# One Strassen block of each row block loaded into w_mod's slots instead of the stage tiles, and some pieces of vector work placed at other chunks

## The chip, the cores and the metric

The kernel runs on one core of one Trainium2 chip. The metric is the device time of one execution in microseconds; the time before is the median of three runs. A profile of one more execution shows where that time goes. Times inside it are counted from the start of its span.

## What is computed

Two residual blocks work on x, a 2048 x 512 array (S x D). The rows `sa, ca, ga, sb, cb, gb` come from `silu(c) @ w_mod`, six slices of 512 columns.

```python
h = layernorm(x) * (1 + ca) + sa
x = x + ga * (Cr @ (h @ Hr.T) - Ci @ (h @ Hi.T))      # DFT over the hidden dim, then over the sequence
h = layernorm(x) * (1 + cb) + sb
z = gelu(h @ w_in)                                    # 1792 columns: z1 | z2, 896 each
g = w_sp @ layernorm(z2) + b_sp[:, None]              # w_sp is 2048 x 2048
x = x + gb * ((z1 * g) @ w_out)
```

`Cr`, `Ci` (2048 x 2048) are the sequence DFT matrices, `Hr`, `Hi` (512 x 512) the hidden ones. All arrays are float32, and the result has to be accurate as float32.

## The kernel before

**Products.** Each float32 operand is split into a rounded high part and the remainder, its low part. `matmul3` (lines 97 to 99) adds three products for every pair: high by high, high by low and low by high. The high part is made by ScalarE (`prep_hi` L266, `hi_unit` L603), the low part by VectorE (`prep_lo` L273, `lo_unit` L607), two steps ahead of the matmuls that use it. The DFT matrices and w_sp must also be turned; VectorE does that from a loaded block with a stream transposition (L538 for the DFT, L231 for w_sp).

**The order of the work is written out by hand.** The kernel is one long list of steps, and every engine executes its own instructions in the order in which they are written. In the DFT a step is called a chunk: 12 matmuls of 128 x 512. `at(n, f, ...)` and `atd(n, f, ...)` hang a piece of work at step n; `run(n)` writes it out right after the matmuls of that step, in the order of registration, and n + 0.5 after the low part of that step. A call hung at a step is therefore not a time: it is a place in the queue of VectorE, ScalarE, SyncE (SP, which issues nearly all loads) and GpSimd (POOL, which issues the stores). A load that waits for its buffer holds every later load on SP.

**The stages.**

| stage | steps | what runs |
|---|---|---|
| a | chunks 0 to 31 | first 512 rows of Cr, Ci by h, plainly |
| t = 1, 2, 3 | 30 chunks each, from 32, 62 and 92 | the other row blocks: 16 chunks of plain products ("k") and 14 of a Strassen-like scheme of seven products ("s") |
| y | 32 chunks from Y0 = 122 | hidden DFT, residual, second layernorm |
| z1, z2 | steps N2 = YE to N2 + 27, then 16 steps to N4 | the two halves of w_in; YE = 154 in chunks |
| w | steps N4 to N4 + 111 | w_sp by z2, seven products in the order 1, 6, 7, 4, 5, 3, 2 |
| o | 16 steps | w_out and the final residual |

Within t the order is: for t = 1 four units of "k" (chunks 32 to 39), 14 chunks "s" (40 to 53), four units "k" (54 to 61); for t = 2 "s" at 62 to 75 and "k" at 76 to 91; for t = 3 "s" at 92 to 105 and "k" at 106 to 121.

**Stage tiles.** A block of 512 x 512 of the DFT matrices is 1 MB, four DMAs by `load_block` (L165). Blocks come through a stream: `src` is the list of all of them, `blocks` holds two buffers with the tag "stage", and `block_done(b)` (called after the second half of block b is turned) loads block b + 2. `CHUNKS` gives the order for t = 1, 2, 3: ("k", t, i) are the four blocks of the plain product, ("s", t, role) the four blocks of the scheme, with roles 11, 12, 21 and 22. `turn_unit(u + 3)` turns a "k" block three units ahead of its use; `turn_s` turns the "s" blocks of t + 1 while t is running, at chunks given in a table. For t = 1 alone the "s" blocks are loaded into another pool, by `load_first`.

**Slots of w_mod.** The pool `raws` has two buffers of 1 MB (`raw(...)`). They hold slices of w_mod (`load_mod`, L310, and `load_columns`), their split copies, the hidden DFT matrices, and pieces of w_sp. A buffer is given to a new tile when, in the written order, its former tile has no reader left; SP then waits until that last reader is done.

**Pieces of w_sp.** The scheme for w_sp needs sums of its quarters. `load_s` (L1055, L1057) loads a piece of 128 rows from three quarters (768 KB in the view of DMAs: one issue of 256 KB and one of 512 KB), `sum_s` computes two sums (L1062, L1063) and then a third (L1066) and stores them (L1069). There are 16 pieces, at the chunks listed in `early`. A fourth sum, for product 3, is made by `load_s4` (L1078) and `sum_s4` (L1082) in eight parts. In the y stage `gate_ht` (L817) multiplies the rows of the hidden DFT matrices by `ga`, and `make_ht` (L827) rounds them.

Of the kernel before, what the change touches and what calls it, by code (L numbers as in the profile page):

```python
# [13 lines left out]
P = 128  # L14
# [5 lines left out]
def fnet_gmlp_kernel(  # L20
# [104 lines left out]
    def at(n, f, *a):  # L125
        fill.setdefault(n, []).append((f, a))
# [6 lines left out]
    def quad(a, r, k):  # L133
        return a[r * Q:(r + 1) * Q, k * Q:(k + 1) * Q]

    TS = (NQ - 1, *range(NQ - 1))
    src = [quad((cr, ci)[j], 0, g) for g in range(NQ) for j in range(2)]
    CHUNKS = {1: (("k", 1, 0), ("k", 1, 1), ("s", 2, 21), ("s", 2, 11), ("s", 2, 12), ("k", 1, 2), ("k", 1, 3), ("s", 2, 22)),
              2: (("s", 3, 21), ("s", 3, 11), ("s", 3, 12), ("k", 2, 0), ("k", 2, 1), ("k", 2, 2), ("s", 3, 22), ("k", 2, 3)),
              3: (("k", 3, 0), ("k", 3, 1), ("k", 3, 2), ("k", 3, 3))}  # L140
    order_b = {}
    for t in range(1, NQ):
        for kind, t_, i in CHUNKS[t]:
            order_b[kind, t_, i] = len(src)
            src.append(quad((cr, ci)[i // 2], t_, i % 2) if kind == "k" else
                       quad((cr, ci)[i % 10 - 1], t_, 1 + i // 10))
    first_s = [quad(cr, 1, 3), quad(cr, 1, 2), quad(ci, 1, 2), quad(ci, 1, 3)]
    NC = len(src)
    src += [None] * (8 * NQ - NC)
    N2 = 4 * len(src)  # L150
    src += [h2_d[t] for t in TS] + h2_d
    FORMS = (1, 2, 6, 7, 4, 5, 3)
# [3 lines left out]
    N4 = N3 + 4 * NQ  # L156
# [5 lines left out]
    def load_block(tile_, a, s0=0, s1=P, engs=(nc.sync,)):  # L162
        v = a.rearrange("(b j) (a s) -> a j b s", j=32, a=4)
        for q in range(4):
            engs[q % len(engs)].dma_start(tile_[32 * q:32 * q + 32, :, s0:s1], v[q][:, :, s0:s1])  # L165
# [134 lines left out]
    def raw(shape, name):  # L300
        return raws.tile(shape, F32, tag="raw", bufs=2, name=name)
# [217 lines left out]
    D1 = 8 * NQ  # L519
    DT = 30  # L520
    Y0 = D1 + 3 * DT
    YE = Y0 + 8 * NQ
# [6 lines left out]
    PH, PL, TP, FT = {}, {}, {}, {}  # L529
# [7 lines left out]
    def turn_pair(dst, st, m):  # L537
        nc.vector.transpose(dst.rearrange("p k (b i) -> p k b i", i=32),  # L538
                            st[:, :, 64 * m:64 * m + 64].rearrange("p b (k i) -> p k b i", k=2))
# [6 lines left out]
    SB = {}  # L546

    def turn_s(t, role, m):

        if m == 0:  # L550
            new_f(t, role)
        if t == 1:
            turn_pair(FT[t, role][:, m], SB[role], m)
        else:
            b = order_b["s", t, role]
            turn_pair(FT[t, role][:, m], stage[b], m)
            if m:
                block_done(b)

    def load_first(role):  # L560
        SB[role] = raw([P, 16, P], f"sb{role}")
        load_block(SB[role], first_s[(21, 11, 12, 22).index(role)])

    def sum_f(t, p, m):

# [479 lines left out]
    def load_s(r, g, b):  # L1045

        if spre:
            t = spre[-1].tile([P, 3, Q], F32, tag="sj", bufs=2, name=f"sj{r}{g}{b}")
        elif n_now[0] not in (85, 86):
            t = raw([P, 3, Q], f"sj{r}{g}{b}")  # L1050
        else:
            t = blocks.tile([P, 3, Q], F32, tag="stage", bufs=2, name=f"sj{r}{g}{b}")
        SJ[r, g, b] = t
        o = r * Q + b * P
        nc.sync.dma_start(t[:, 0], w_sp[o:o + P, g * Q:(g + 1) * Q])  # L1055
        v = w_sp.rearrange("r (j c) -> r j c", j=2)[S // 2 + o:S // 2 + o + P]
        nc.sync.dma_start(t[:, 1:], v[:, :, g * Q:(g + 1) * Q])  # L1057
# [240 lines left out]
    n_now = [0]  # L1298

    def atd(n, f, *a):  # L1300

        at(("d", n) if n < YE else N2 + int(n - YE), f, *a)
# [16 lines left out]
    for s, n in ((8, 10), (9, 10)):  # L1319
        m = n + (s == 9)  # L1320
# [13 lines left out]
        fpool.append(tf.enter_context(pool("fpool", "right")))  # L1334

    for role, l, n, m in ((21, 12, 16, 18), (11, 14, 20, 22), (12, 23, 28.5, 30), (22, 30.5, 35, 36)):
        atd(l, load_first, role)
        atd(n, turn_s, 1, role, 0)
        atd(m, turn_s, 1, role, 1)
    for n, *todo in ((23, (change_f,), (sum_v, 5)), (24, (hi_v, 5)), (25, (lo_v, 5), (sum_v, 7), (sum_v, 6)),  # L1340
# [6 lines left out]
    for t in range(1, NQ):  # L1347
        o = D1 + DT * (t - 1)
        d = 8 if t == 1 else 0
        for m in range(2):  # L1350
            atd(o + d + 0.5 + m, sum_f, t, 6, m)
            atd(o + d + 6 + m, sum_f, t, 3, m)
        for j in range(2):
            atd(o + ((22, 29) if t == 1 else (21, 29))[j], *((out_last, j) if t == NQ - 1 else (out_k, t, j)))
        if t < NQ - 1:
            for role, n, m in (((21, 13, 14), (11, 15.5, 16.5), (12, 17.5, 18.5), (22, 24, 25)) if t == 1 else
                               ((21, 3, 5), (11, 7.5, 8.5), (12, 9.5, 10.5), (22, 21, 23))):
                atd(o + n, turn_s, t + 1, role, 0)
                atd(o + m, turn_s, t + 1, role, 1)
            for p, n, m in (((5, 26, 26.5), (7, 27, 28)) if t == 1 else ((5, 24, 26), (7, 27, 28))):  # L1360
                atd(o + n, sum_f, t + 1, p, 0)
                atd(o + m, sum_f, t + 1, p, 1)
# [7 lines left out]

    atd(33, row_c)
    atd(38, silu_c)
    for j, l, n in ((1, 66, 73), (0, 67, 77)):
        atd(l, load_columns, j)
        for k in range(4):
            atd(n + k, weigh_column, j, k)
            atd(n + k + 1, sum_column, j, k)
    atd(82, scale_columns)
    for j, l, ns, m, k, plus_one in ((2, 37, (40, 41, 42), 44, 6, False), (4, 46, (56, 57, 58), 60, 3, True),
                                     (3, 58.5, (63, 64, 65), 66, 7, False), (5, 78, (82, 83, 85), 87, 0, False)):  # L1380
        atd(l, load_mod, j)
        atd(ns[0], sum_mod, j, [0, 1])
        atd(ns[1], sum_mod, j, [2, 3])
        atd(ns[2], split_mod, j)
        atd(m, spread_mod, j, k, plus_one)
    early = ((43.5, 53), (85.5, 89), (86.5, 91), (109, 113), (117, 120))
    early += tuple((YE + c, YE + c + 4) for c in (14, 17, 20, 23, 27, 29, 31, 33, 35, 37, 38))
    for (n, m), u in zip(early, [(r, g, b) for g in range(2) for b in range(4) for r in range(2)]):
        atd(n, load_s, *u)
        atd(m, sum_s, *u, True)  # L1390
        atd(m + 1, sum_s, *u, False)
    atd(93, load, order_b["k", 3, 0])
    atd(96.5, load, order_b["k", 3, 1])
    hrs = ctx.enter_context(ExitStack())
    o = D1 + 2 * DT
# [9 lines left out]
    for n, *todo in ((-6, (load_ht, 0)), (-3, (turn_ht, 0, 0)), (-2, (turn_ht, 0, 1)), (-1, (turn_ht, 0, 2)), (0, (turn_ht, 0, 3)), (8, (scale_w0, 0)),  # L1405
                     (9, (load_ht, 1), (weigh_ht, 0, 0), (weigh_ht, 0, 1)), (10, (weigh_ht, 0, 2), (weigh_ht, 0, 3), (load_w0, 0)),
                     (12, (fold_ht, 0, 0), (fold_ht, 0, 1)), (13, (fold_ht, 0, 2), (fold_ht, 0, 3)),
                     (14, (open_hr,), (split_acc, 0), (turn_ht, 1, 0), (scale_w0, 1), (read_row, 2, hrp)),
                     (15, (change_y,), (turn_ht, 1, 1), (turn_ht, 1, 2), (read_row, 4, yp), (read_row, 3, yp)),
                     (16, (turn_ht, 1, 3), (weigh_ht, 1, 0), (load_w0, 1)),  # L1410
                     (17, (weigh_ht, 1, 1), (weigh_ht, 1, 2), (load_xr, YORD[0])),
                     (18, (weigh_ht, 1, 3), (load_xr, YORD[1])),
                     (19, (gate_ht, 0, 2), (gate_ht, 0, 3), (make_ht, 0, 2), (make_ht, 0, 3)), (20, (fold_ht, 1, 2), (fold_ht, 1, 3)),
                     (21.5, (make_ht_lo, 0, 2), (gate_ht, 1, 2)), (22, (gate_ht, 1, 3), (make_ht, 1, 2), (make_ht, 1, 3), (fold_ht, 1, 0)),
                     (23, (split_acc, 1), (fold_ht, 1, 1), (gate_ht, 0, 1)), (24, (make_ht_lo, 1, 2), (gate_ht, 1, 1)),
                     (25, (spread_acc, 0, 0), (spread_acc, 1, 1), (row_ht, 0), (row_ht, 1), (gate_ht, 0, 0), (gate_ht, 1, 0)),
                     (26, (make_ht, 0, 0), (make_ht, 0, 1), (make_ht_lo, 0, 0)),
                     (27, (make_ht, 1, 0), (make_ht, 1, 1), (make_ht_lo, 1, 0))):
        for f, *a in todo:
            atd(o + n, f, *a)  # L1420
    for i, m in enumerate(YORD):
        n, e = (Y0 + i, Y0 + 4 + i) if i < 4 else (Y0 + 2 * i, Y0 + 2 * i + 1)
# [47 lines left out]
    n = 0  # L1470
# [44 lines left out]
    for i, p in enumerate(PROD):  # L1515
        for k in range(8):
            n = NB[p] + 2 * k
# [36 lines left out]
            at(NB[2] + 7 + f, make_u, 7, 0, f)  # L1554
    at(NB[2] + 8, load_z1, 4, 1)
    at(NB[2] + 11, load_z1, 7, 1)
    for n, u in zip((4, 8, 12, 15, 49, 52, 55, 58), [(r, g, h) for g in range(2) for h in range(2) for r in range(2)]):
        at(N4 + n - 4, load_s4, *u)
        at(N4 + n, sum_s4, *u)
    for f in range(NF):  # L1560
        n = NB[6] + 3 * f
        at(n - 3, load_wo, f)
# [65 lines left out]
```

## Time and profile before

| | us |
|---|---|
| median of 3 runs | 951.37 (948.83 to 957.2) |
| the profiled execution | 952.62 |
| its span | 950.5 |
| TensorE busy | 930.6 |
| VectorE busy | 745.9 |
| ScalarE busy | 433.0 |
| mean granted TensorE clock | 0.994 |

The chain of work that ended last lies 79% on TensorE, 6% on DMA and 5% on VectorE. The DMA engines moved 178.82 MB, 188 GB/s over the span.

How to read the rows: PE is TensorE's matmuls, PEld its weight loads, DVE is VectorE, ACT ScalarE, POOL GpSimd, SPq the DMA issues of SyncE. A row of the timeline gives its start, its duration, the engine, the line of the kernel, the operation, what it writes and reads, and in brackets the idle time of that engine before it and what ended it. A row of the windows gives a stretch, its length, the busy time of PE, PEld, DVE, ACT and POOL with the number of instructions, then the granted clock of TensorE (1.00 is full), the busy share of the DMA engines (over 1 where they are full) and GB/s. A row of the waits gives the waiting engine, tile and line, what it waited for, the total in us, how often, and the longest.

### The profile page before, as it was taken

How to read it: one execution, taken by the hardware profiler on the slowest of the kernel's cores; microseconds unless marked ns; L12 is line 12 of the kernel's file. 1: busy time of each engine (PE TensorE's matmuls, PEld its weight loads, DVE VectorE, ACT ScalarE, POOL GpSimd, SP SyncE). 2: the span in 40 equal slices, each digit the busy share in tenths (PEclk: the TensorE clock that was granted, in tenths of full speed). 3: DMA queues.
4: the chain of work that ended last, by engine and by line, in shares of the span. 5: the costliest groups of instructions: out<-in, count | busy, mean ns of one | idle time of the engine just before them, and what ended most of it. 6: DMA issues, size and time to landing. Idle time of an engine off the chain costs nothing.

```text
span 950.5 us, 12132 instructions
## 1 busy us (share of the span) xinstructions
PE 930.6 (98%) x4088; PEld 769.7 (81%) x4088; DVE 745.9 (78%) x1016; ACT 433.0 (46%) x686; POOL 157.2 (17%) x312
## 2 busy tenths in 40 slices
PE   8999999998999999999999999999999999999998
PEld 6788877886878878787787999887888888888886
DVE  7779687898797993877778677877789788885872
ACT  3485343353335344662875456553544444331221
POOL 1330001100020002643423354201000000000000
PEclk9999999998999999999999999999999999999999
DMA  8998929877685826685898877696659756833641
GB/s 200 216 209 190 215 59 225 226 144 148 167 251 100 232 89 178 214 270 181 206 346 296 236 217 229 199 266 166 163 124 247 214 125 137 207 93 126 193 160 59
DMA packets 269374, 178.82 MB, mean 188 GB/s; under 512 B 135168, under 2 KB 233728, under 8 KB 269184
## 3 DMA queue, kind: packets, MB, share of 16 engines
q1 hardware_dynamic: 253744, 133.99, 58.7%
q0 software_dynamic: 12576, 41.44, 11.5%
q10 hardware_dynamic: 2992, 2.62, 1.1%
q8 instruction: 32, 0.52, 0.2%
q14 instruction: 30, 0.25, 0.1%
HBM read 135.01 MB, written 43.00 MB: 187 GB/s over the span
## 4 chain that ended last, share of the span: by engine, by line
PE 79%; DMA 6%; DVE 5%; issue 4%; SPq 2%; POOL 2%; ACT 1%; POOLq 0%; DVEq 0%; ACTq 0%
PE gw L98 9%; PE gw L99 9%; PE gw L97 9%; PE gs_c L98 3%; PE gs_c L99 3%; PE gs_c L97 3%; PE z2p L99 3%; PE z2p L98 3%; PE z2p L97 3%; PE op L98 3%; PE op L97 3%; PE op L99 3%; PE gs_u L98 2%; DMA stage<-in_A_dft_seq_im_dram 2%; PE gs_u L99 2%
## 5 line engine op out<-in xcount | busy, mean ns | idle before, releaser
L98 PE MATMUL gw<-al,bh 128*128 128x512 f32 x400 | 155.8, 390 | 1.7 <-DVE al L273 1.7
L99 PE MATMUL gw<-ah,bl 128*128 128x512 f32 x400 | 155.6, 389 | 0.0
L97 PE MATMUL gw<-ah,bh 128*128 128x512 f32 x400 | 155.6, 389 | 0.0
L273 DVE TENSOR_TENSOR al<-t,ah 128x512 fp32r<-128x512 f32 x136 | 92.5, 686 | 54.7 <-PE gw L98 27.8
L266 ACT ACTIVATE ah<-t 128x512 fp32r<-128x512 f32 x136 | 84.8, 626 | 98.5 <-PE gw L99 44.7
L98 PEld LDWEIGHTS gw<-al,bh 128*128 128x128 f32 x400 | 75.1, 188 | 17.9 <-DVE al L273 2.4
L97 PEld LDWEIGHTS gw<-ah,bh 128*128 128x128 f32 x400 | 75.1, 188 | 15.7
L99 PEld LDWEIGHTS gw<-ah,bl 128*128 128x128 f32 x400 | 75.1, 188 | 15.5
L231 DVE STREAM_TRANSPOSE t<-stage 128x1024 f32<-128x1024 f32 x56 | 69.4, 1239 | 0.9 <-DMA stage<-in_B_w_sp_dram 0.9
L603 ACT ACTIVATE ph<-f 128x1024 fp32r<-128x1024 f32 x42 | 44.4, 1058 | 40.4 <-PE gs_c L99 12.4
L607 DVE TENSOR_TENSOR pl<-f,ph 128x1024 fp32r<-128x1024 f32 x42 | 50.7, 1214 | 11.5 <-ACT ph L603 11.4
L603 ACT ACTIVATE ph<-tp 128x1024 fp32r<-128x1024 f32 x35 | 36.9, 1053 | 48.0 <-DVE tp L538 18.7
L1105 ACT ACTIVATE bh<-z 128x512 fp32r<-128x512 f32 (+1 forms) x56 | 32.8, 585 | 56.1 <-PE gw L98 52.5
L98 PE MATMUL gs_c<-pl,hh 128*128 128x512 f32 x144 | 56.4, 392 | 0.9 <-DVE pl L607 0.9
L97 PE MATMUL gs_c<-ph,hh 128*128 128x512 f32 x144 | 56.3, 391 | 0.0
L99 PE MATMUL gs_c<-ph,hl 128*128 128x512 f32 x144 | 56.3, 391 | 0.0
L538 DVE STREAM_TRANSPOSE tp<-stage 128x1024 f32<-128x1024 f32 x36 | 44.4, 1234 | 13.8 <-DMA stage<-in_A_dft_seq_im_dram 9.3
L1069 POOL DMA_DIRECT2D s_d<-sj x48 | 26.5, 552 | 135.4 <-DVE sj L1062 93.3
L98 PE MATMUL z2p<-wil,ah 128*128 128x448 f32 x128 | 46.7, 365 | 0.0
L97 PE MATMUL z2p<-wih,ah 128*128 128x448 f32 x128 | 46.7, 365 | 0.0
L99 PE MATMUL z2p<-wih,al 128*128 128x448 f32 x128 | 46.7, 365 | 0.0
L607 DVE TENSOR_TENSOR pl<-tp,ph 128x1024 fp32r<-128x1024 f32 x35 | 42.3, 1209 | 5.5 <-ACT ph L603 5.5
(288 smaller groups left out, 2238.2 us busy)
## 6 DMA issues: line engine op xcount, KB each, us to landing
stage<-s_d SPq DMA_DIRECT2D x128, 128.0 KB, 3.0
stage<-in_A_dft_seq_re_dram SPq DMA_DIRECT2D x52, 256.0 KB, 6.3
stage<-in_A_dft_seq_im_dram SPq DMA_DIRECT2D x52, 256.0 KB, 5.5
s_d<-sj POOLq DMA_DIRECT2D x48, 256.0 KB, 4.6
stage<-in_B_w_sp_dram SPq DMA_DIRECT2D x96, 128.0 KB, 3.5
sj<-in_B_w_sp_dram SPq DMA_DIRECT2D x16, 512.0 KB, 6.2
stage<-h_d SPq DMA_DIRECT2D x32, 256.0 KB, 7.3
gr<-g_d SPq DMA_DIRECT2D x12, 512.0 KB, 5.9
```

Source lines behind the costliest of these rows:

```text
L97: nc.tensor.matmul(acc, ah, bh, start=first, stop=False, skip_group_check=go_on)
L98: nc.tensor.matmul(acc, ah, bl, start=False, stop=False, skip_group_check=go_on)
L99: nc.tensor.matmul(acc, al, bh, start=False, stop=last, skip_group_check=go_on)
L231: nc.vector.transpose(t.rearrange("p r (b i) -> p r b i", i=32), st[:, :, :, 16 * k:16 * k + 32])
L266: nc.scalar.activation(AH[n], source(n), AF.Copy)
L273: nc.vector.tensor_tensor(AL[n], source(n), AH[n].bitcast(F32), op=ALU.subtract)
L538: nc.vector.transpose(dst.rearrange("p k (b i) -> p k b i", i=32), st[:, :, 64 * m:64 * m + 64].rearrange("p b (k i) -> p k b i", k=2))
L603: nc.scalar.activation(pair_of(PH, u, "ph"), source_unit(u), AF.Copy)
L607: nc.vector.tensor_tensor(pair_of(PL, u, "pl"), source_unit(u), PH[u].bitcast(F32), op=ALU.subtract)
L1069: nc.gpsimd.dma_start(s_d[m, r, g][b * P:(b + 1) * P, :], a)
L1105: nc.scalar.activation(BH[p, k][:, :w], b_of(p, k), AF.Copy)
```

## The change

- The blocks ("s", 2, 12) and ("s", 3, 12) are taken out of the stage stream. `load_sb` (formerly `load_first`) loads them into a buffer of `raws` at chunk 43 and at chunk 65.5. Every later block of the stream moves one place (for t = 3 two places) forward.
- In `raws` other loads make room: the first piece of w_sp goes out at 44.5 instead of 43.5, slice 4 of w_mod at 51 instead of 46, its columns 1 at 66.5 and columns 0 at 73 (instead of 66 and 67, the second set weighed from 78 instead of 77), slice 5 at 77.5 instead of 78.
- The pieces of w_sp: the fourth moves from 109 (load) and 113 (sum) to 112.5 and 115.5, and into a stage tile; the fifth leaves the DFT; the twelve that follow have their own list of loads and sums, and from YE + 27 on all three sums of a piece stand at one step.
- `make_ht` of two pairs of rows stands one chunk later.
- The fourth sums of product 3 have their own loads and sums.

```diff
@@ stage stream
+    def quad_s(t, role):
+        return quad((cr, ci)[role % 10 - 1], t, 1 + role // 10)
-    CHUNKS = {1: (("k", 1, 0), ("k", 1, 1), ("s", 2, 21), ("s", 2, 11), ("s", 2, 12), ("k", 1, 2), ("k", 1, 3), ("s", 2, 22)),
-              2: (("s", 3, 21), ("s", 3, 11), ("s", 3, 12), ("k", 2, 0), ("k", 2, 1), ("k", 2, 2), ("s", 3, 22), ("k", 2, 3)),
+    CHUNKS = {1: (("k", 1, 0), ("k", 1, 1), ("s", 2, 21), ("s", 2, 11), ("k", 1, 2), ("k", 1, 3), ("s", 2, 22)),
+              2: (("s", 3, 21), ("s", 3, 11), ("k", 2, 0), ("k", 2, 1), ("k", 2, 2), ("s", 3, 22), ("k", 2, 3)),
...
@@ turn_s
-        if t == 1:
-            turn_pair(FT[t, role][:, m], SB[role], m)
+        if (t, role) in SB:
+            turn_pair(FT[t, role][:, m], SB[t, role], m)
...
-    def load_first(role):
-        SB[role] = raw([P, 16, P], f"sb{role}")
-        load_block(SB[role], first_s[(21, 11, 12, 22).index(role)])
+    def load_sb(t, role):
+        SB[t, role] = raw([P, 16, P], f"sb{t}_{role}")
+        load_block(SB[t, role], quad_s(t, role))
@@ load_s
-        elif n_now[0] not in (85, 86):
+        elif n_now[0] < D1 + DT:
             t = raw([P, 3, Q], f"sj{r}{g}{b}")
@@ chunks of the DFT, o = D1 + DT * (t - 1)
-        atd(l, load_first, role)
+        atd(l, load_sb, 1, role)
...
+            atd(o + (11 if t == 1 else 3.5), load_sb, t + 1, 12)
...
-    for j, l, n in ((1, 66, 73), (0, 67, 77)):
+    for j, l, n in ((1, 66.5, 73), (0, 73, 78)):
         atd(l, load_columns, j)
...
-    atd(82, scale_columns)
-    for j, l, ns, m, k, plus_one in ((2, 37, (40, 41, 42), 44, 6, False), (4, 46, (56, 57, 58), 60, 3, True),
-                                     (3, 58.5, (63, 64, 65), 66, 7, False), (5, 78, (82, 83, 85), 87, 0, False)):
+    atd(83, scale_columns)
+    for j, l, ns, m, k, plus_one in ((2, 37, (40, 41, 42), 44, 6, False), (4, 51, (56, 57, 58), 60, 3, True),
+                                     (3, 58.5, (63, 64, 65), 66, 7, False), (5, 77.5, (82, 83, 85), 87, 0, False)):
         atd(l, load_mod, j)
...
-    early = ((43.5, 53), (85.5, 89), (86.5, 91), (109, 113), (117, 120))
-    early += tuple((YE + c, YE + c + 4) for c in (14, 17, 20, 23, 27, 29, 31, 33, 35, 37, 38))
+    early = ((44.5, 53), (85.5, 89), (86.5, 91), (112.5, 115.5))
+    early += tuple((YE + n, YE + m) for n, m in ((14, 17), (15, 19), (19, 27), (21, 28), (28, 31), (29, 33), (32, 35),
+                                                 (34, 37), (36, 39), (38, 41), (39, 42), (41, 44)))
     for (n, m), u in zip(early, [(r, g, b) for g in range(2) for b in range(4) for r in range(2)]):
         atd(n, load_s, *u)
         atd(m, sum_s, *u, True)
-        atd(m + 1, sum_s, *u, False)
+        atd(m + (m < YE + 23), sum_s, *u, False)
@@ gated rows, o = 92
-                     (19, (gate_ht, 0, 2), (gate_ht, 0, 3), (make_ht, 0, 2), (make_ht, 0, 3)), (20, (fold_ht, 1, 2), (fold_ht, 1, 3)),
-                     (21.5, (make_ht_lo, 0, 2), (gate_ht, 1, 2)), (22, (gate_ht, 1, 3), (make_ht, 1, 2), (make_ht, 1, 3), (fold_ht, 1, 0)),
-                     (23, (split_acc, 1), (fold_ht, 1, 1), (gate_ht, 0, 1)), (24, (make_ht_lo, 1, 2), (gate_ht, 1, 1)),
+                     (19, (gate_ht, 0, 2), (gate_ht, 0, 3)), (20, (fold_ht, 1, 2), (fold_ht, 1, 3), (make_ht, 0, 2), (make_ht, 0, 3)),
+                     (21.5, (make_ht_lo, 0, 2), (gate_ht, 1, 2)), (22, (gate_ht, 1, 3), (fold_ht, 1, 0)),
+                     (23, (make_ht, 1, 2), (make_ht, 1, 3), (split_acc, 1), (fold_ht, 1, 1), (gate_ht, 0, 1)), (24, (make_ht_lo, 1, 2), (gate_ht, 1, 1)),
@@ fourth sums
-    for n, u in zip((4, 8, 12, 15, 49, 52, 55, 58), [(r, g, h) for g in range(2) for h in range(2) for r in range(2)]):
-        at(N4 + n - 4, load_s4, *u)
-        at(N4 + n, sum_s4, *u)
+    for (n, m), u in zip(((0, 6), (4, 10), (11, 16), (14, 20), (43, 48), (46, 52), (52, 56), (56, 60)),
+                         [(r, g, h) for g in range(2) for h in range(2) for r in range(2)]):
+        at(N4 + n, load_s4, *u)
+        at(N4 + m, sum_s4, *u)
```

More of the change, by code (lines that the diff above doesn't have):

```diff
@@ L144, in fnet_gmlp_kernel @@
             order_b[kind, t_, i] = len(src)
-            src.append(quad((cr, ci)[i // 2], t_, i % 2) if kind == "k" else
-                       quad((cr, ci)[i % 10 - 1], t_, 1 + i // 10))
-    first_s = [quad(cr, 1, 3), quad(cr, 1, 2), quad(ci, 1, 2), quad(ci, 1, 3)]
+            src.append(quad((cr, ci)[i // 2], t_, i % 2) if kind == "k" else quad_s(t_, i))
     NC = len(src)
```

## The prediction

> **What bounds the kernel now.** I read the head of the page first, then TensorE's row in the view of waits.
>
> ```profile
> span 950.5 us, 12132 instructions
> PE 930.6 (98%) x4088; PEld 769.7 (81%) x4088; DVE 745.9 (78%) x1016; ACT 433.0 (46%) x686; POOL 157.2 (17%) x312
> ...
> PE gs_u L98 <- DVE pl L607: 6.9, 3, 3.3
> ```
>
> TensorE sets the end: 930.6 of 950.5 us are busy, and no matmul is added or removed. The change can only act on the gaps (20 us, some at the start and end) and on the clock after them. The largest waits are three for `pl`, the low half that VectorE makes of an operand. So I went through the timeline of TensorE for rows with an idle time, with the rows where neighbouring steps begin:
>
> ```profile
> 152.61 0.39 PE L97 MATMUL gs_u<-ph,hh 128*128 128x512 f32 x1
> 157.82 0.50 PE L98 MATMUL gs_u<-pl,hh 128*128 128x512 f32 x1 [2.11 <-DVE pl L607]
> 163.40 0.39 PE L97 MATMUL gs_c<-ph,hh 128*128 128x512 f32 x1
> 189.75 0.39 PE L97 MATMUL gs_v<-ph,vh 128*128 128x512 f32 x1
> 195.19 0.39 PE L97 MATMUL gs_u<-ph,vh 128*128 128x512 f32 x1
> 217.43 0.39 PE L97 MATMUL gs_u<-ph,hh 128*128 128x512 f32 x1
> 223.88 0.79 PE L98 MATMUL gs_u<-pl,hh 128*128 128x512 f32 x1 [3.34 <-DVE pl L607]
> 232.11 0.39 PE L97 MATMUL gs_c<-ph,hh 128*128 128x512 f32 x1
> 348.69 0.49 PE L98 MATMUL gs_u<-pl,hh 128*128 128x512 f32 x1 [1.50 <-DVE pl L607]
> 514.47 0.47 PE L97 MATMUL z1p<-ah,w 128*128 128x512 f32 x1 [1.29 <-DVE z1k L999]
> 647.49 0.50 PE L98 MATMUL gw<-al,bh 128*128 128x512 f32 x1 [1.65 <-DVE al L273]
> ```
>
> From 189.75 to 195.19 run two undisturbed chunks of 12 matmuls: 5.44 us, so 0.227 us a matmul and 2.72 us a chunk. From 152.61 to 163.40 (chunks 52, 53 and half of 54) run 30 matmuls, 6.80 us of work in 10.79: 3.99 lost, though the gap shows 2.11. From 217.43 to 232.11 run 36, 8.16 us in 14.68: 6.52 lost against a gap of 3.34. The rest is clock, as the stretches by windows show (column before last but one, PEclk):
>
> ```profile
> 158.00:160.00 2.00, 2.00 (x6) 1.60 (x7) 2.00 (x2) 0.68 (x1) 0.00 (x0) 0.59 0.03 9
> 647.00:649.00 2.00, 1.51 (x7) 1.24 (x8) 2.00 (x3) 1.31 (x3) 0.25 (x1) 1.00 1.05 348
> ```
>
> After the gap of 2.11 the granted clock is 0.59; after that of 1.65 it stays 1.00. These two stalls are 10.5 us; the three smaller ones are 4.4 together.
>
> **Part 1: blocks s2_12 and s3_12 leave the stage stream.** The stage tiles are two buffers; a load starts when the block two places earlier is turned. The first stall on VectorE's and SP's timelines:
>
> ```profile
> 138.84 1.93 SPq L165 DMA_DIRECT2D stage<-in_A_dft_seq_im_dram  x4
> 145.64 15.22 SPq L165 DMA_DIRECT2D stage<-in_A_dft_seq_im_dram  x12
> ...
> 144.37 1.23 DVE L538 STREAM_TRANSPOSE f<-stage 128x1024 f32<-128x1024 f32 x1
> 150.09 1.24 DVE L538 STREAM_TRANSPOSE f<-stage 128x1024 f32<-128x1024 f32 x1
> 155.42 1.25 DVE L538 STREAM_TRANSPOSE tp<-stage 128x1024 f32<-128x1024 f32 x1 [4.09 <-DMA stage<-in_A_dft_seq_im_dram]
> 156.59 1.18 DVE L607 TENSOR_TENSOR pl<-f,ph 128x1024 fp32r<-128x1024 f32 x1
> ```
>
> The load at 138.84 is s2_12 (1 MB). The block that chunk 51 turns, ("k",1,2), could be issued only at 145.64, when the turn at 144.37 freed its buffer, and VectorE stood 4.09 us before it; the `pl` of chunk 53 queues behind it. With s2_12 gone, ("k",1,2) takes the place of 138.84, 6.8 us earlier, and lands at about 148.6 (155.42 - 6.8), before VectorE is free at 151.3 (150.09 + 1.24). The `pl` comes 4.1 us earlier, at 152.5, for a chunk that begins at 155.33 (152.61 + 2.72). s2_12 itself is issued at chunk 43 into w_mod's slot that "mod" 2 left at chunk 42, six chunks before its turn; its four DMAs take 1.9 us of SP's queue (as at 138.84), and behind them stands only the w_sp piece, which was moved to 44.5 and is not summed before chunk 53. ("mod" 4, moved from 46 to 51, waits on SP until that turn frees the slot, at 151.3; queued behind it is block s2_22, not needed before chunk 56 at 163.5.) Gain: **4.0 us**, the whole loss.
>
> The second stall:
>
> ```profile
> 197.26 1.92 SPq L165 DMA_DIRECT2D wb<-in_w_mod_dram  x4
> 200.68 2.14 SPq L165 DMA_DIRECT2D stage<-in_A_dft_seq_im_dram  x4
> 202.99 4.38 SPq L165 DMA_DIRECT2D wb<-in_w_mod_dram  x4
> 210.30 8.09 SPq L165 DMA_DIRECT2D stage<-in_A_dft_seq_re_dram  x8
> 243.62 1.92 SPq L165 DMA_DIRECT2D stage<-in_A_dft_seq_im_dram  x4
> ...
> 214.91 1.24 DVE L538 STREAM_TRANSPOSE f<-stage 128x1024 f32<-128x1024 f32 x1
> 220.13 1.25 DVE L538 STREAM_TRANSPOSE tp<-stage 128x1024 f32<-128x1024 f32 x1 [3.98 <-DMA stage<-in_A_dft_seq_re_dram]
> 222.61 1.22 DVE L607 TENSOR_TENSOR pl<-f,ph 128x1024 fp32r<-128x1024 f32 x1
> 250.79 1.25 DVE L538 STREAM_TRANSPOSE tp<-stage 128x1024 f32<-128x1024 f32 x1 [4.64 <-DMA stage<-in_A_dft_seq_im_dram]
> ```
>
> Here four megabytes queue up: w_mod's two columns around s3_12, then ("k",2,0) at 210.30, which lands at 220.1 although VectorE is free at 216.1. The window at 218 shows how full the engines are:
>
> ```profile
> 218.00:220.00 2.00, 2.00 (x11) 1.65 (x10) 0.00 (x0) 0.00 (x0) 0.00 (x0) 1.00 1.24 221
> ```
>
> At 221 GB/s a block of 1.05 MB takes 4.7 us. After the change s3_12 goes out at 197.3 (chunk 65.5), one column behind it (66.5), and ("k",2,0) at 200.7 in s3_12's old place; the other column waits until chunk 73. In the old order ("k",2,0) is the fourth block: 197.3 + 18.8 = 216.1, and it landed 4.0 later, sharing the engines with its successor. In the new order it is the third: 211.4, so it lands between 213 and 215.4, before 216.1. The stall at its place goes. But VectorE now becomes the limit: from turn to `pl` it needs 2.48 us (220.13 to 222.61: the turn and one weighed column of 1.3), plus 1.2 for the `pl`, 3.7 a chunk against TensorE's 2.72 in chunks 73 to 75. Before, it ran without a break from 220.13 to the turn that releases the load at 243.62, while a TensorE at half clock waited for it. Starting at 216.1 (4.0 earlier), and with one column of 1.3 now behind that turn (the second set begins at 78, not 77), the load goes out at 238.3 and lands at 245.5 (it took 250.79 - 243.62 = 7.2), 5.3 us earlier than now. Bounds: 6.5 if nothing is left, 0 if ("k",2,0) lands at 220. I take **5.3 us**, because the rows of VectorE leave no break in between.
>
> A rule to weigh. The Trainium skill (TensorE: Matmul & The Clock Gate, "HAM oscillation — how this bites in real kernels") has a gap lower the clock when it exceeds about 3.4 us. By that rule the gap of 2.11 would have cost its own length and the first gain would be 2.1, the sum 1.9 smaller. The row at 158.00 contradicts it: 0.59 after 2.11 us.
>
> **Part 2: w_sp pieces and gated rows before the fourth product.** The stall at 348.69 waits for a `pl` that VectorE begins late:
>
> ```profile
> 337.89 0.68 DVE L1062 TENSOR_TENSOR sj<-sj 128x512 f32<-128x512 f32 x1
> 347.42 1.22 DVE L607 TENSOR_TENSOR pl<-tp,ph 128x1024 fp32r<-128x1024 f32 x1
> ```
>
> Three such `sj` operations stand in chunks 113 and 114; they move to 115.5 and 116.5, behind that `pl`, which so comes about 2.0 us earlier (3 x 0.68). `make_ht` (ScalarE) moves behind nothing that TensorE needs before chunk 122. The gap of 1.50 goes; the same 2.0 us now stand ahead of the last `pl` (chunk 120), which I let cost 0.1 (bounds 0 to 1.5). The load at 112.5 takes a stage buffer, freed by a turn in chunk 111; `out_last` wants both buffers at chunk 121, and the piece's writes are out by then, 4.5 chunks after the last sum. The pieces of chunks 117 to 121 leave, work that lay beside TensorE: nothing. Gain **1.4**.
>
> **Part 3: the pieces under the first gMLP product (offsets from YE).** The first sum moves from 18 to 17, but its load does not move.
>
> ```profile
> 489.23 1.31 SPq L1055 DMA_DIRECT2D sj<-in_B_w_sp_dram  x1
> 498.05 0.69 DVE L1062 TENSOR_TENSOR sj<-sj 128x512 f32<-128x512 f32 x1 [3.33 <-DMA sj<-in_B_w_sp_dram]
> 499.39 1.08 DVE L900 TENSOR_TENSOR wil<-wraw,wih 128x896 fp32r<-128x896 f32 x1
> 500.39 0.68 DVE L273 TENSOR_TENSOR al<-hz,ah 128x512 fp32r<-128x512 f32 x1
> ...
> 499.65 0.39 PE L98 MATMUL z1g<-al,w 128*128 128x512 f32 x1
> ```
>
> SP is behind loads of h2 until 489.23, and the piece lands at 498. Already now VectorE stands 3.33 us. One chunk earlier, the same wait has a `wil` and the `al` of step 20 queued behind it: sum 498.05 to 499.4, `wil` to 500.4, `al` done at 501.1. TensorE's second matmul of step 20 needs it at 499.65: **1.45 us** of new gap. The eight matmuls left end at 502.9, so step 21 wants its `al` at 503.1; ahead of it stand the sum's third part and a second `wil` (1.6), so it is done at 503.3: 0.2 more. Step 22 wants its own nine matmuls later, at 505.3; two parts of the second sum and a `hz` subtraction (2.6) stand ahead, and it is done at 506.4: 1.1 more. New loss 2.7 (bounds 0, if the piece lands 3 us earlier, and 5, if 2 us later). The sums that stood in 24 and 25 leave; so the `z1k` additions begin three operations (2.0) earlier and the gap of 1.29 goes. The other pieces lie in steps of the second product, where TensorE's timeline has no gap; nothing. Net **-1.4**.
>
> **Part 4: the fourth sums.**
>
> ```profile
> 645.01 1.23 DVE L1082 TENSOR_TENSOR s<-s 128x1024 f32<-128x1024 f32 x1 [5.49 <-DMA s<-s_d]
> ```
>
> This wait leads to the gap of 1.65 at 647.49. Its load moves 3 chunks back, its sum 5: 5.4 us more between them, against a wait of 5.49. Gain **1.65** (bounds 0 to 1.65); the later four only shift by chunks without a gap.
>
> Sum: 4.0 + 5.3 + 1.4 - 1.4 + 1.65 = **11.0 us**. The profiled execution took 952.62 (its span and 2.1 around it), 1.25 above the median of 951.37; so 941.6 there, **940.4** for the median.
>
> **Rivals.** *Nothing left over*: the piece at 489 lands in time and VectorE keeps up in chunks 73 to 79: 4.0 + 6.5 + 1.4 + 1.3 + 1.65 = 14.9, 936.5. For: each needs only 1 to 3 us. Against: SP is held by the same loads. *The second stall stays*: the bytes from 197 on are the same, and 8.09 us for two blocks at 210.30 shows SP slowed by full queues; if ("k",2,0) lands at 220, 5.3 is lost again: 945.7. *The stall only changes its block*: the later loads, ("k",1,3) or ("k",2,2), are late by as much; only parts 2 to 4 count, 1.6: 949.7. Against: they land 2 to 4 us ahead by the reckoning above. *Slower*: the moved sum at step 17. Every microsecond by which its piece lands after 498 is a microsecond of gap at step 20, and past about 2 us the clock falls and doubles it (2.11 became 3.99). The other parts bring 12.4 and the `z1k` gap pays for the small ones behind, so it decides from a landing 5 us later (gap 6.4, 12.9 with the clock); at 7 us the gap is 8.45, the price 16.9 and the time 951.4 + 4.5 = 956. For: SP's queue is full there, and the four later pieces wait one behind another; against: nothing is put ahead of that load.
>
> **How the numbers follow.** Forecast 0.50, nothing left over 0.14, second stall stays 0.20, changed block 0.09, slower 0.07. A measurement tells about 1% (9.5 us) from no change; 941.9 is the edge. The forecast, uncertain by 2 to 3 us, lies below it in two thirds of its cases: 0.34 + 0.14 + 0.02 of the second rival = 0.50 faster. Of the slower rival 0.04 I give to landings so late that it loses over 1%; 0.46 is left within. The range from 934.5 to 948.5 leaves out the last two rivals and little else.
>
> **What would show it.** Right: no row with a gap in chunks 50 to 60 and the clock 1.00 there; turn of ("k",2,0) not ended by a DMA; 36 matmuls from chunk 74 in under 10 us; a new gap of `z1g` on `al` at step 20; none on `z1k` or after the fourth `s` sum. Wrong: a gap over 2 us anywhere in the first 280 us, or SP's load of ("k",1,2) not 6 us earlier against TensorE.

## The result and the profile after

The changed kernel takes 942.26 us (median of 6 runs, 938.07 to 945.11). The kernel before, run beside it on the same chip, takes 953.68 (6 runs, 948.83 to 957.95). The ratio is 0.988, with a 95% interval from 0.9837 to 0.9923: about 1.2% faster, 11.4 us. The profiled execution of the changed kernel took 942.02 us at a mean granted clock of 0.998. The head of its page, and TensorE's rows of its waits:

```profile
span 940.3 us, 12142 instructions
PE 927.7 (99%) x4088; PEld 768.2 (82%) x4088; DVE 746.6 (79%) x1016; ACT 433.4 (46%) x686; POOL 158.6 (17%) x312
...
PE z1g L98 <- DVE al L274: 2.2, 1, 2.2
PE gs_c L98 <- DVE pl L608: 1.1, 1, 1.1
PE gs_u L98 <- DVE pl L608: 0.7, 1, 0.7
```

Line numbers are mostly one higher than before. The wait of `gs_u` fell from 6.9 us in three places to 0.7 in one. `z1g` is new. TensorE is busy 2.9 us less with the same 4088 matmuls: it spends less time at a low clock. In TensorE's timeline these rows have the gaps:

```profile
246.97 0.50 PE L98 MATMUL gs_u<-pl,hh 128*128 128x512 f32 x1 [0.69 <-DVE pl L608]
267.97 0.50 PE L98 MATMUL gs_c<-pl,hh 128*128 128x512 f32 x1 [1.15 <-DVE pl L608]
490.97 0.73 PE L98 MATMUL z1g<-al,w 128*128 128x512 f32 x1 [2.17 <-DVE al L274]
```

**Where the time came from.** Both kernels execute the same matmuls in the same order, so I compared the start of the same matmul in the two timelines. How much earlier it is in the kernel after, stage by stage:

| stretch | won there, us | forecast |
|---|---|---|
| start of the program | 0.67 | none |
| first stall (chunks 52 to 54) | 3.99 | 4.0 |
| second stall (chunks 74 to 76, less the gap of chunk 86) | 5.34 | 5.3 |
| chunks 92 to 95 | -0.26 | none |
| before the fourth product (chunks 116 to 120) | 1.84 | 1.4 |
| y | -0.54 | none |
| z1 | -2.54 | -1.4 |
| w | 1.79 | 1.65 |

Together that is 10.3; the spans differ by 10.2 (950.5 to 940.3). The table compares one execution of each kernel with one of the other. The first stall in the profile after, on TensorE, VectorE and SP:

```profile
151.92 0.39 PE L97 MATMUL gs_u<-ph,hh 128*128 128x512 f32 x1
158.72 0.39 PE L97 MATMUL gs_c<-ph,hh 128*128 128x512 f32 x1
...
149.40 1.24 DVE L539 STREAM_TRANSPOSE f<-sb 128x1024 f32<-128x1024 f32 x1
150.56 1.20 DVE L539 STREAM_TRANSPOSE tp<-stage 128x1024 f32<-128x1024 f32 x1
...
138.15 8.70 SPq L166 DMA_DIRECT2D stage<-in_A_dft_seq_im_dram  x8
150.67 1.77 SPq L311 DMA_DIRECT2D wm<-in_w_mod_dram  x4
```

The 30 matmuls from chunk 52 take 6.80 us, their bare work. The turn of k(1,2) at 150.56 carries no bracket: VectorE goes straight from one turn to the next. Two things differ ahead of it: the load is issued at 138.15, and w_mod's slice 4 goes out at 150.67 and not at 140.82. Both are part of the change, so this profile can't say which of them did it. The second stall:

```profile
198.09 10.25 SPq L166 DMA_DIRECT2D stage<-in_A_dft_seq_re_dram  x8
233.53 1.92 SPq L166 DMA_DIRECT2D stage<-in_A_dft_seq_im_dram  x4
...
211.43 1.20 DVE L539 STREAM_TRANSPOSE tp<-stage 128x1024 f32<-128x1024 f32 x1
240.52 1.25 DVE L539 STREAM_TRANSPOSE tp<-stage 128x1024 f32<-128x1024 f32 x1 [3.38 <-DMA stage<-in_A_dft_seq_im_dram]
```

Add the 4.68 us by which TensorE is already ahead there: the turn of k(2,0) stands at 216.1, the last block's load at 238.2 and its turn at 245.2. The prediction had 216.1, 238.3 and 245.5. At step 20 of z1, on VectorE and in the windows:

```profile
487.89 0.69 DVE L1063 TENSOR_TENSOR sj<-sj 128x512 f32<-128x512 f32 x1 [6.90 <-DMA sj<-in_B_w_sp_dram]
489.23 1.08 DVE L901 TENSOR_TENSOR wil<-wraw,wih 128x896 fp32r<-128x896 f32 x1
490.23 0.69 DVE L274 TENSOR_TENSOR al<-hz,ah 128x512 fp32r<-128x512 f32 x1
```

```profile
490.00:492.00 2.00, 1.03 (x3) 0.85 (x4) 2.00 (x4) 0.08 (x1) 2.00 (x5) 0.77 0.85 342
492.00:494.00 2.00, 2.00 (x6) 1.60 (x5) 1.97 (x4) 0.00 (x0) 0.81 (x2) 0.50 0.98 385
```

VectorE stands 6.90 us before the piece (3.33 in the kernel before), with `wil` and `al` queued behind it, in the order forecast. The gap is 2.17, and behind it the granted clock is 0.50. The 66 matmuls of this `z1g` take 19.04 us in place of 14.96: 4.08 lost, 1.91 of them beyond the gap, most of that by the clock.

### The profile page after: what moved, and what is told of

Read it like the earlier page. It is cut to its first block, busy times and chain, and to the rows that moved or that the text cites. A ratio compares the mean times of both kernels' runs of the same rounds, so it can differ in the third digit from the quotient of the medians.

```text
span 940.3 us, 12142 instructions
## 1 busy us (share of the span) xinstructions
PE 927.7 (99%) x4088; PEld 768.2 (82%) x4088; DVE 746.6 (79%) x1016; ACT 433.4 (46%) x686; POOL 158.6 (17%) x312
## 4 chain that ended last, share of the span: by engine, by line
PE 71%; issue 11%; DVE 7%; DMA 5%; POOL 2%; SPq 1%; ACT 1%; DVEq 0%; ACTq 0%; POOLq 0%
PE gw L98 9%; PE gw L99 9%; PE gw L97 9%; PE op L99 3%; PE op L98 3%; PE op L97 3%; PE gp L98 2%; PE gp L99 2%; PE gp L97 2%; PE z2p L97 2%; PE z2p L99 2%; PE z2p L98 2%; PE gs_c L98 2%; PE gs_c L99 2%; PE gs_c L97 2%
```

## The experiments

**1. The parts apart.** The kernel after with the pieces of w_sp, the gated rows and the fourth sums put back as before; the two blocks and the loads of w_mod stay as changed.

```diff
-    early = ((44.5, 53), (85.5, 89), (86.5, 91), (112.5, 115.5))
-    early += tuple((YE + n, YE + m) for n, m in ((14, 17), (15, 19), (19, 27), ...
+    early = ((44.5, 53), (85.5, 89), (86.5, 91), (109, 113), (117, 120))
+    early += tuple((YE + c, YE + c + 4) for c in (14, 17, 20, 23, 27, 29, 31, 33, 35, 37, 38))
...
```

> The kernel after with parts 2 to 4 undone: the blocks s2_12 and s3_12 in w_mod's slots, and the w_mod loads and the first w_sp piece where that puts them. If the parts add up as the two traces read (first stall 4.0, second 5.3), this is 9.3 us under the kernel before; the gaps of 1.5, 1.3 and 1.65 us in the later stages come back, and the 2.2 us gap of z1g on al at step 20 is absent. Rival: the later edits are needed for the gain (they free VectorE or SP for the blocks); then less than 5 us.

Measured: 945.0 us, ratio 0.9903 (0.987 to 0.9936). The first stall brings 3.99, the second 5.3. The three smaller gaps are back, and there is none at step 20 of `z1g`. TensorE's timeline:

```profile
339.89 0.51 PE L98 MATMUL gs_u<-pl,hh 128*128 128x512 f32 x1 [1.50 <-DVE pl L608]
505.20 0.47 PE L97 MATMUL z1p<-ah,w 128*128 128x512 f32 x1 [1.69 <-DVE z1k L1000]
639.38 0.50 PE L98 MATMUL gw<-al,bh 128*128 128x512 f32 x1 [2.79 <-DVE al L274]
```

So up to chunk 91 the parts do not act on one another: 9.2 us are won there, 9.3 in the kernel after. Behind it the profiled execution loses more than the kernel before: its gap in chunk 93 is 2.10 (0.89 before) and that before `gw` 2.79 (1.65 before), and it ends 6.7 us shorter. By the medians the blocks and w_mod's loads bring 9.3 us; the rest is small and of both signs.

**2. w_mod's loads without the blocks.** The kernel before with only w_mod's loads at their new chunks. This keeps both blocks in the stage stream, so no block is freed earlier; only the megabytes of w_mod stand behind other loads.

```diff
-    for j, l, n in ((1, 66, 73), (0, 67, 77)):
+    for j, l, n in ((1, 66.5, 73), (0, 73, 78)):
...
-    ... (4, 46, (56, 57, 58), 60, 3, True), ... (5, 78, (82, 83, 85), 87, 0, False)):
+    ... (4, 51, (56, 57, 58), 60, 3, True), ... (5, 77.5, (82, 83, 85), 87, 0, False)):
```

> The kernel before with only the w_mod loads moved (slice 4 from 46 to 51, columns 1 to 66.5, columns 0 from 67 to 73 and weighed from 78, slice 5 to 77.5); both blocks stay in the stage stream. Theory A, the place in the stream decides: block k(1,2) still goes out only when the turn of chunk 48.5 frees its buffer, so the first stall stays above 1.5 us and the second above 2, and the time is within 3 us of before. Rival B, the queue decides: what made the loads late was the megabyte of w_mod ahead of each in the DMA queues (k(1,2) took 9.6 us from issue to turn where 7 are usual). Then both gaps fall under 0.7 us, the clock stays at 1.00, and the kernel gains 7 to 9 us with no block moved.

Measured: 948.19 us, ratio 0.9941 (0.9917 to 0.9965). SP's issues, VectorE's two turns that waited for DMAs, and TensorE's gaps:

```profile
137.63 14.42 SPq L165 DMA_DIRECT2D stage<-in_A_dft_seq_im_dram  x12
152.15 2.31 SPq L310 DMA_DIRECT2D wm<-in_w_mod_dram  x4
...
151.33 1.25 DVE L538 STREAM_TRANSPOSE tp<-stage 128x1024 f32<-128x1024 f32 x1 [1.21 <-DMA stage<-in_A_dft_seq_im_dram]
214.05 1.25 DVE L538 STREAM_TRANSPOSE tp<-stage 128x1024 f32<-128x1024 f32 x1 [1.03 <-DMA stage<-in_A_dft_seq_re_dram]
...
188.40 0.50 PE L98 MATMUL gs_v<-pl,vh 128*128 128x512 f32 x1 [0.44 <-DVE pl L607]
192.12 0.50 PE L98 MATMUL gs_u<-pl,vh 128*128 128x512 f32 x1 [0.70 <-DVE pl L607]
217.81 0.50 PE L98 MATMUL gs_u<-pl,hh 128*128 128x512 f32 x1 [0.40 <-DVE pl L607]
221.42 0.50 PE L98 MATMUL gs_c<-pl,hh 128*128 128x512 f32 x1 [0.57 <-DVE pl L607]
```

The first stall is gone whole (3.99 us won), with the block still in its old place in the stream: it waits 1.21 and not 4.09, which TensorE does not feel. Most of the second is gone too, 4.9 of 6.5. But 2 us are lost in chunks 64 to 66, where before there was no gap. By chunk 91 this kernel has won 6.3 us, the changed one 9.3. So the order of the queues, w_mod's megabyte ahead of the block, made the first stall; the move of the blocks adds about 3 us.

**3. Slice 4 alone.** The kernel before with slice 4 at chunk 51. (A first execution of this kernel took 4145 us, with TensorE slow from start to end. Nothing here explains it, and it tells nothing of the edit; the runs told here are later ones.)

```diff
-    ... (4, 46, (56, 57, 58), 60, 3, True), ...
+    ... (4, 51, (56, 57, 58), 60, 3, True), ...
```

> The kernel before with one edit: w_mod's slice 4 is loaded at chunk 51 and not 46, nothing else; the blocks stay where they are, and so do the other two loads of w_mod. Theory Q (the queues' order made the first stall: slice 4's megabyte, issued before block k(1,2), is what held it): the turn of k(1,2) comes 3 us or more earlier against TensorE's matmuls, the gap of 2.11 us goes, and the 30 matmuls from chunk 52 take 6.8 and not 10.8 us; the second stall keeps most of its 6.5 us, since its columns are slices 5 and 6, which do not move. Time about 4 us under before, ratio 0.996. Rival S (stream position: the block can't go out earlier than its buffer is freed at chunk 50, so it lands late all the same): a gap over 1 us stays in chunk 53, and the time is within 2 us of before. In between (a gap under 1 us) both have a share.

Measured: 951.97 us, ratio 0.9987 (0.9959 to 1.0014). Here are the gaps of TensorE, and a turn on VectorE (`hr`, of the hidden DFT matrix):

```profile
191.57 0.50 PE L98 MATMUL gs_u<-pl,vh 128*128 128x512 f32 x1 [0.71 <-DVE pl L607]
218.92 0.50 PE L98 MATMUL gs_u<-pl,hh 128*128 128x512 f32 x1 [2.03 <-DVE pl L607]
251.89 0.50 PE L98 MATMUL gs_u<-pl,hh 128*128 128x512 f32 x1 [1.14 <-DVE pl L607]
273.93 0.50 PE L98 MATMUL gs_c<-pl,hh 128*128 128x512 f32 x1 [2.18 <-DVE pl L607]
...
265.47 0.71 DVE L187 STREAM_TRANSPOSE hr<-hraw 128x512 f32<-128x512 f32 x1 [3.65 <-DMA hraw<-in_A_dft_hid_re_dram]
```

In place theory Q holds: no row with a gap stands in chunk 53, and the 30 matmuls take 6.80 us. In time it does not: the ratio allows at most 4 us, and 1 is likelier. Matmul by matmul, the 4.0 won are followed by 1.5 lost in chunks 64 to 66, 2.6 won at the second stall (4.0 lost there, not 6.5), 1.1 lost at chunk 86 and 2.9 in chunks 92 to 95, where the gap of 2.18 takes the clock to 0.58. Then 2.5 go in y and z1. So in this execution the gain was real and was given back. Not all that was lost need come of it, though: in chunks 92 to 95 `hraw` is issued at the same distance from TensorE's matmuls as in the kernel before and only lands 1.8 us later, and that landing differs from one execution to the next (experiment 4).

**4. The sum at step 18.** The kernel after with the first two pieces under z1 summed one step later, the first where it was before.

```diff
-    early += tuple((YE + n, YE + m) for n, m in ((14, 17), (15, 19), (19, 27), ...
+    early += tuple((YE + n, YE + m) for n, m in ((14, 18), (15, 20), (19, 27), ...
```

> The kernel after with the first two w_sp sums under the first gMLP product one step later (18 and 20, not 17 and 19); nothing else. Theory: the new gap of 2.17 us at step 20, and the 4.08 us lost there with the clock, come from the al that queues behind the sum's wait on VectorE. Then it is gone, or under 0.4 us, and the span is 3.7 to 4.1 us shorter than after. Rival: the piece's landing itself (0.85 us later than before relative to TensorE) is what costs, and the wait only moves to step 21: a gap of 1 us or more stays and at most 2 us are won.

Measured: 940.35 us, ratio 0.9858 (0.9834 to 0.9882). TensorE's timeline has

```profile
269.66 0.50 PE L98 MATMUL gs_c<-pl,hh 128*128 128x512 f32 x1 [2.37 <-DVE pl L608]
492.90 0.50 PE L98 MATMUL z1g<-al,w 128*128 128x512 f32 x1 [0.61 <-DVE al L274]
```

The loss of the 66 matmuls is 1.22 us and not 4.08. So 2.86 came from the moved sum. That is less than the 3.7 of the theory, for a gap of 0.61 has moved on to step 21. The profiled execution had lost as much before that, though: chunks 92 to 95 cost 4.26 us here and 1.45 in the kernel after, behind the wait for `hraw` known from experiment 3 (3.39 us on VectorE here, 2.61 in the kernel after). Up to there the two kernels are written alike, so this is a difference between two executions and not between two orders. The median gained some 2 us, with intervals that overlap.

**5. The same load twice.** The kernel after, in which the larger issue of that first piece is made twice over, so that it lands later. This prices the slower rival.

```diff
-            nc.sync.dma_start(t[:, 1:], v[:, :, g * Q:(g + 1) * Q])
+            for _ in range(2 if (r, g, b) == (0, 0, 2) else 1):
+                nc.sync.dma_start(t[:, 1:], v[:, :, g * Q:(g + 1) * Q])
```

> The kernel after, with the larger load (512 KB) of the first w_sp piece under the first gMLP product issued twice into the same place, so that it lands later by one more transfer; the data stay the same. Rival of the prediction that ends slower: each microsecond of landing is a microsecond of gap at step 20, and the clock doubles it. If the second transfer takes about 3 us, the gap goes from 2.2 to about 5 us. Theory D, loss is twice the gap: 10 us lost there instead of 4.1, span 6 us longer than after. Theory E, the clock's part does not grow with the gap (it was 1.9 after the gaps of 2.1 and 2.2, 3.2 after 3.3): 7 to 8 us lost, span 3 to 4 longer.

Measured in one run: 946.24 us. TensorE, and the windows before and at its return:

```profile
495.51 0.80 PE L98 MATMUL z1g<-al,w 128*128 128x512 f32 x1 [6.89 <-DVE al L274]
```

```profile
493.00:495.00 2.00, 0.00 (x0) 0.00 (x0) 1.97 (x4) 0.00 (x0) 1.39 (x3) 0.50 0.84 308
495.00:497.00 2.00, 1.49 (x4) 1.20 (x5) 2.00 (x4) 0.00 (x0) 2.00 (x5) 0.50 0.85 340
```

The gap grew by 4.72, as much as the piece's delay against TensorE (4.7): one for one. But the 66 matmuls lost 8.56 us, so 1.67 went beyond the gap, no more than the 1.91 behind a gap of 2.17. The clock had already fallen to 0.50 while TensorE had no matmul. The clock's part does not double the gap.

**6. VectorE spread evenly.** Experiment 4 with the columns weighed two at a time at chunks 76 to 82, and slice 5 at 78.5: is the gap at chunk 86 left by VectorE's load, or by the time that the last block's load takes?

```diff
-    for j, l, n in ((1, 66.5, 73), (0, 73, 78)):
+    for j, l, n in ((1, 66.5, 76), (0, 73, 80)):
...
-            atd(n + k, weigh_column, j, k)
-            atd(n + k + 1, sum_column, j, k)
+            atd(n + k // 2 * 2, weigh_column, j, k)
+            atd(n + k // 2 * 2 + 0.5, sum_column, j, k)
```

> As e3_sum18, and the eight weighed columns of w_mod stand two at a time in chunks 76, 78, 80 and 82 (slice 5 loaded at 78.5), so that VectorE has no column beside a turn and a pl in chunks 73 to 75. Theory: what was left of the second stall (0.3 us at chunk 76 and 0.7 at chunk 86) is VectorE's own work; then both gaps go and the span is 1.0 us shorter than e3_sum18. Rival: the latency of the last block's load, 7 us from a fixed turn, sets the second of them; then the gap before chunk 86 stays within 0.3 us of 0.7.

Measured: 940.53 us, ratio 0.9862 (0.9835 to 0.9888), no better than experiment 4. The second stall itself goes whole (6.52 won), but the gap at chunk 86 grows:

```profile
247.55 0.50 PE L98 MATMUL gs_u<-pl,hh 128*128 128x512 f32 x1 [1.51 <-DVE pl L608]
...
241.10 1.25 DVE L539 STREAM_TRANSPOSE tp<-stage 128x1024 f32<-128x1024 f32 x1 [1.50 <-DMA stage<-in_A_dft_seq_im_dram]
```

The load that this turn waits for goes out at 233.88, 7.2 us ahead. It is k(2,3), released by a turn that is tied to the matmuls; so what is won at chunk 76 is lost at 86. The rival is right here about the cause, though the gap is larger than the 1.0 that it allowed.

**7. The last block earlier.** Experiment 4 with k(2,3) ahead of s(3,22) in the stream, the latter turned one chunk later.

```diff
-              2: (... ("k", 2, 2), ("s", 3, 22), ("k", 2, 3)),
+              2: (... ("k", 2, 2), ("k", 2, 3), ("s", 3, 22)),
...
-                               ... (22, 21, 23))):
+                               ... (22, 23, 24))):
```

> As e3_sum18, and in the stream of t = 2 the block k(2,3) goes before s(3,22), whose two turns move from chunks 83 and 85 to 85 and 86. Theory: what is left of the second stall before chunk 86 (0.85 us in e3_sum18, 1.5 in e4_even) is the load of k(2,3), issued by the turn of chunk 81 and 7.2 us under way, two chunks before it is turned. Issued by the turn of chunk 77 instead, it lands before chunk 82: VectorE's wait of 3.5 us and the gap are gone, 0.7 to 0.9 us shorter than e3_sum18 up to chunk 91. Rival, VectorE's own work is the limit: the gap stays within 0.3 us, only without a wait for a DMA ahead of it.

Measured: 937.56 us, ratio 0.9829 (0.9804 to 0.9854). The turn of k(2,3) on VectorE carries no bracket, and TensorE has no gap at chunk 86:

```profile
237.08 1.24 DVE L539 STREAM_TRANSPOSE tp<-stage 128x1024 f32<-128x1024 f32 x1
```

Up to chunk 91 that wins 1.2 us over experiment 4. It does something else as well: SP comes to `hraw` 1.7 us earlier against TensorE, VectorE's wait for it falls to 2.04 and the gap in chunk 93 to 0.89.

**8. `hraw` ahead of the piece.** Experiment 7 with the second piece of w_sp loaded at 86.5, behind `hraw`, to take the wait of chunks 92 to 95 away.

```diff
-    early = ((44.5, 53), (85.5, 89), (86.5, 91), (112.5, 115.5))
+    early = ((44.5, 53), (86.5, 89), (86.5, 91), (112.5, 115.5))
```

> As e6_swap, and the load of the hidden DFT matrix (1 MB) is issued ahead of the second w_sp piece (768 KB) and not behind it (the piece at 86.5 instead of 85.5). Theory: the gap in chunks 92 to 95, 0.9 us before the change, 1.15 after it, 2.1 and 2.4 in e1_blocks and e3_sum18, starts with VectorE's wait for that matrix (3.2 to 3.4 us) and differs from run to run with its landing; 2 us earlier, the wait falls under 1.5 us and the gap under 0.5. Rival: the pieces' sums, not the matrix, fill VectorE there; then the gap stays at 1 us or more.

Measured: 936.62 us, ratio 0.9818 (0.9791 to 0.9845), the fastest version, though its interval and that of experiment 7 overlap. The wait for `hraw` is gone, and VectorE stands 2.50 us before the piece instead; TensorE's gap is the same 0.89 as in experiment 7:

```profile
256.04 0.69 DVE L1063 TENSOR_TENSOR sj<-sj 128x512 f32<-128x512 f32 x1 [2.50 <-DMA sj<-in_B_w_sp_dram]
266.23 0.50 PE L98 MATMUL gs_c<-pl,hh 128*128 128x512 f32 x1 [0.89 <-DVE pl L608]
```

So the theory behind this edit fell: what is left of that gap does not come from `hraw`'s wait. VectorE's rows in experiment 7 show where it comes from:

```profile
262.27 1.37 DVE L723 TENSOR_TENSOR um<-gs_c,um 128x512 f32<-128x512 f32 x2 [0.66 <-PE gs_c L99]
...
265.51 1.18 DVE L608 TENSOR_TENSOR pl<-f,ph 128x1024 fp32r<-128x1024 f32 x1
```

VectorE waits for TensorE here, so it has made up for `hraw` by then, and from `um` to `pl` (two sums of a piece and a turn of `hr` lie between) it works without a break: these operations set the 0.89. The kernel before has the same gap with a wait of 1.82 for `hraw`. Where the wait is longer, `um` has no bracket and the gap grows with it: 1.15 after 2.61 (the kernel after), 1.75 after 3.22 (experiment 6), 2.10 after 3.51 (experiment 1), 2.18 after 3.65 (experiment 3). So the theory holds for what lies above 0.89, and experiment 7 had already taken that away.

## Why the prediction was right, and where it was not

**The sum.** 11.0 was forecast. The medians differ by 11.4, the two profiled executions by 10.6, of which 0.67 is at the start, which the change does not touch. What was left out (chunks 92 to 95, y) lost 0.8. The forecast of 940.4 stands 1.9 under the measured 942.26; the kernel before, run again, was itself 2.3 above the median on which it rested. That the total fits so well is in part luck: part 3 and the stages left out brought 1.9 less than the sum has for them, the start and parts 2 and 4 brought 1.3 more. The signs named beforehand came: no gap in chunks 50 to 60, 36 matmuls from chunk 74 in 8.63 us, the new gap of `z1g` at step 20, none on `z1k` or behind the fourth sums.

**Part 1, first stall: size right, reason incomplete.** 4.0 against 3.99. The prediction gave it all to the block's place in the stream, 6.8 us earlier. Experiments 2 and 3 show that the move of slice 4 alone is enough, with the place unchanged. Two rows tell it. Before, the block went out at 145.64, behind w_mod's megabyte (issued from 140.82), and its turn began 9.8 later. In experiment 2 it went out behind no such megabyte, and its turn began 4.1 earlier; 1.2 of that is only the start of the program. The prediction read slice 4's move as harmless and asked only what waits behind it, not what it stops holding up. Whether the place alone would also do could not be tried: the block's slot is free only if slice 4 moves. The view of DMAs bears on it, though; its last number is the median time from issue to landing of the four parts of a block. The rows are s2_12 in the kernel before, with slice 4 issued right behind it, and k(1,2) there, with slice 4 ahead of it (in experiment 2 its number is 4.5 too):

```profile
stage<-in_A_dft_seq_im_dram SPq DMA_DIRECT2D x4, 256.0 KB, 4.5
stage<-in_A_dft_seq_im_dram SPq DMA_DIRECT2D x4, 256.0 KB, 6.9
```

A megabyte behind the block did not hold it up, one ahead of it did. By these rows the earlier place would have been enough by itself too, as the prediction had it; no run shows that.

**Part 1, second stall: right by its own steps.** 5.3 against 5.34, and the three moments agree within 0.3 us. VectorE was the limit, and experiment 6 bears that out: relieved of its columns, it regains the whole 6.5. What experiment 6 adds is that the load of k(2,3) is a second limit directly behind, so the bound of 6.5 was not to be had by VectorE's work alone; experiment 7 had to move the load.

**Part 2** brought 1.84 against 1.4. The gap of 1.50 went; the last `pl` cost 0.21 against the 0.1 allowed. Right.

**Part 3 was mis-sized: -2.54 against -1.4.** The mechanism is the one described: wait, `wil`, `al`, gap at step 20. Two terms were off. The piece landed 0.85 us later against TensorE than the 498.05 assumed (487.89 and the 11.01 by which TensorE was ahead give 498.90), and the gap was 2.17 rather than 1.45. And past the gap the clock fell to 0.50, for which the sum had no term (a gap of 1.45 would have had none: the row of 1.65 shows the clock at 1.00). Together 4.08 lost rather than 2.7. The 0.2 and 1.1 put down for steps 21 and 22 did not show on their own; the lower clock gave VectorE the time. The `z1k` gap went as forecast (1.54 back, 1.3 expected).

**Part 4** brought 1.79 against 1.65. Right.

**The rivals.** *The second stall stays* did not happen, and *the stall only changes its block* only as 0.71 us at chunk 86. The slower rival's place was right; experiment 5 made its landing 4.7 us later still, and the run was still under the time before. Its price was wrong: "doubles it" should have been "adds about 2 us" for a gap of that length. With 8.45 of gap it would, by that estimate, have cost some 10.1 and not 16.9.

**The rule on the clock.** The Trainium skill (TensorE: Matmul & The Clock Gate, "HAM oscillation — how this bites in real kernels") asks for a gap above about 3.4 us. The runs here contradict it once more: 0.50 after 2.17, 0.58 after 2.18, 0.75 over the window that holds 2.03.

```profile
218.00:222.00 4.00, 3.08 (x9) 2.47 (x10) 3.96 (x5) 2.17 (x5) 0.00 (x0) 0.75 0.26 61
274.00:278.00 4.00, 4.00 (x11) 3.13 (x12) 4.00 (x5) 0.58 (x1) 0.54 (x1) 0.58 1.04 305
```

(Both windows are of experiment 3.) Nor does the length alone decide near 2 us: after gaps of 2.01 (experiment 2) and 2.10 (experiment 1), both in chunk 93, the clock stayed at 1.00. Of experiment 1:

```profile
268.88 0.50 PE L98 MATMUL gs_c<-pl,hh 128*128 128x512 f32 x1 [2.10 <-DVE pl L608]
...
270.00:272.00 2.00, 2.00 (x11) 1.63 (x10) 2.00 (x3) 0.85 (x2) 0.27 (x1) 1.00 1.09 345
```

**What stays open.** The loss of 0.5 in y was not followed up. The 0.3 in chunks 92 to 95 goes with `hraw`'s longer wait; why that load lands more than 1 us later in one execution than in another of the same order is not known. That VectorE's own operations make the gap of 0.89 is read from the rows, without a run that takes one away. Why a gap of 2.10 left the clock alone and one of 2.03 did not is open.

## What to carry to other kernels

When a load is late, ask what else entered the queues just before it: moving a megabyte that is not yet needed behind the urgent one can be the whole remedy. A stall removed in a chain of hand-placed loads is a promise only: the next load that is tied to something else takes it back, so count the gain at the end of the stage and not at the stall. Price a gap of more than some 2 us as its length plus one drop of the clock (1.7 to 3.2 us here), and not as twice its length.

## What the runs showed of the hardware

What a drop of TensorE's clock costs is not in proportion to the gap that brings it. Beyond the gap itself, 1.9 us were lost after each of the gaps of 2.03, 2.11, 2.17, 2.18, 2.37 and 2.79, 3.18 after 3.34 and 1.67 after 6.89. Where the clock stayed full, gaps of 1.50 to 2.10 cost 0.3 to 0.5 beyond their length. There is no sharp border: every gap from 1.50 to 2.01 left the clock full and every gap from 2.11 on lowered it, while of two in between 2.10 left it and 2.03 lowered it.

The block k(1,2), 1 MB, took 9.6 us to land behind another megabyte (the kernel before) and 6.7 to 6.9 with none just ahead of it (the kernel after, experiments 2 and 3). The block s2_12 took 6.9 with a megabyte issued right behind it.
